# A 16 KB store of zeros to the output ahead of all loads, in a group normalisation kernel bound by DMA

## The chip, the cores and the metric

The kernel runs on 1 core of one Trainium2 chip. The metric is device time in microseconds (us). In the first measurement the kernel before took 635.31 us (median of 3 runs, 635.22 to 635.34).

## The reference, cut to what matters

```python
# x: (128, 1024, 32, 16) bf16;  g, b: (1024,) bf16;  32 groups of 32 channels
xr  = x.reshape(B, 32, 32, H, W)
mu  = xr.mean(axis=(2, 3, 4), keepdims=True)
var = ((xr - mu) ** 2).mean(axis=(2, 3, 4), keepdims=True)
xn  = ((xr - mu) / jnp.sqrt(var + 1e-5)).reshape(B, C, H, W)
return xn * g[None, :, None, None] + b[None, :, None, None]
```

The input has 134.2 MB, and so has the output. Each byte is read once and written once.

## The kernel before

The kernel works on 32 tiles of 4 MB. A tile is 128 rows of 16,384 bf16 elements (32 KB a row): four samples times 32 groups, one group of one sample in each row. A tile is loaded into one of six buffers, its sums are taken on TensorE, its squares on ScalarE (ACT), it is scaled in place on VectorE (DVE), GpSimd (POOL) and ACT, and it is stored from the same buffer. All large loads and stores are issued from SyncE (SP) and go through one queue, q1. Six tiles are loaded ahead; the stores of tiles 0 and 1 come behind those six loads. From there on loads and stores alternate.

```python
XBUFS = 6
UPFRONT = 6
AHEAD = 5
...
    def L(i):                                  # load of tile i
        xt = xpool.tile([P, F], BF16, name="xt")
        parts = NQ if i == 0 or i >= NT - 1 else 1
        w = F // parts
        for c in range(parts):
            chain("sp", nc.sync.dma_start(
                out=xt[:, c * w : (c + 1) * w], in_=x_v[i][:, c * w : (c + 1) * w]))
        state[i] = {"xt": xt}

    for i in range(min(UPFRONT, NT)):
        L(i)

    gb_b = consts.tile([G, 2, KC], BF16)
    chain("act", nc.scalar.dma_start(out=gb_b[:, 0, :], in_=g_v))
    chain("act", nc.scalar.dma_start(out=gb_b[:, 1, :], in_=b_v))
...
    def S(i, lo, hi):                          # store of tile i
        chain("sp", nc.sync.dma_start(
            out=o_v[i][:, lo * QF : hi * QF], in_=state[i]["xt"][:, lo * QF : hi * QF]))
...
    def finish(i):                             # cut: the last two tiles go in parts
        for k in range(KC - LAST_SHARE, KC):
            scale_on("act", i, k)
        S(i, 0, NQ)
        state.pop(i)
        j = i + AHEAD
        if UPFRONT <= j < NT:
            L(j)
```

The `chain` helper only fixes the order on one engine. Line breaks are changed here and the rest is cut.

Of the kernel before, what the change touches and what calls it, by code (L numbers as in the profile page):

```python
# [11 lines left out]
BF16 = mybir.dt.bfloat16  # L12
# [17 lines left out]
def kernel(  # L30
# [13 lines left out]
    nc = tc.nc  # L44
# [11 lines left out]
    MMN = MM_FREE  # L56
# [8 lines left out]
    o_v = out.rearrange("(t n) (g k) h w -> t (n g) (k h w)", n=NS, g=G)  # L65
# [3 lines left out]
    consts = ctx.enter_context(tc.tile_pool(name="consts", bufs=1))  # L69
# [15 lines left out]
    def chain(key, inst):  # L85
        prev = last.get(key)
        if prev is not None:
            tc.add_manual_dep(inst.ins, prev.ins.name, nosync, reason="pipeline order")
        last[key] = inst
        return inst  # L90
# [3 lines left out]
    def L(i):  # L94
# [4 lines that stand above are left out]
            chain(  # L99
                "sp",  # L100
                nc.sync.dma_start(  # L101
                    out=xt[:, c * w : (c + 1) * w], in_=x_v[i][:, c * w : (c + 1) * w]
                ),
            )
        state[i] = {"xt": xt}

    for i in range(min(UPFRONT, NT)):
        L(i)
# [13 lines left out]
        out=eye[:],  # L122
        in_=ones_b[:],
# [8 lines left out]
        out=rep[:].rearrange("q (n a) -> q n a", n=NS),  # L132
        in_=ones_b[0:G, :].rearrange("q (n a) -> q n a", n=NS),
# [274 lines left out]
    def finish(i):  # L408
        if i < 0 or in_parts(i):
            return  # L410
# [7 lines that stand above are left out]
# [42 lines left out]
```

## Time and profile before

| what | before |
|---|---|
| device time, median of all 6 runs | 635.26 us |
| span of the profiled run | 633.4 us |
| busiest compute engine, ACT | 82% |
| bytes moved, mean rate over the span | 268.69 MB, 424 GB/s |
| one 32 KB packet on a DMA engine (median) | 1.21 us |

The page of the kernel before: the busy digits and the rate by slices (40 equal slices of the span; 9 is 90% or more), the DMA queues, and the chain of waits that ended last.

```profile
DMA  9999999999999999999999999999999999999995
GB/s 367 433 431 419 430 431 430 430 433 430 430 434 433 435 431 429 431 430 428 431 435 426 433 439 439 431 426 433 430 435 430 430 435 430 433 423 439 431 418 228
...
q1 hardware_dynamic: 10944, 268.44, 98.8%
q8 instruction: 8, 0.13, 0.1%
q14 instruction: 14, 0.11, 0.0%
q10 hardware_dynamic: 96, 0.00, 0.0%
...
DMA 71%; ACT 10%; PE 9%; DVE 3%; issue 3%; POOL 1%; SPq 0%; DVEq 0%; ACTq 0%; POOLq 0%
```

The DMA engines are full from the second slice to the last but one. So a faster compute engine should not help here; fewer microseconds of DMA time should. The queue lines give packets, MB and share. q10 is ACT's queue and carries only g and b here.

The sum behind this uses the packet records of the trace. 7,680 packets of 32 KB at 1.213 us and 2,048 of 8 KB at 0.309 us, over 16 engines, make 621.8 us of data per engine, starting at 1.8 us.

Two further readings of the trace carry the argument. First, the windows view shows a dip where the six loads ahead end. Its columns are the window, its length, the busy time (and count) of PE, PEld, DVE, ACT and POOL, the TensorE clock, the DMA share, and GB/s. Packets are counted where they start, so short windows swing by some per cent.

```profile
17.00:23.00 6.00, 0.10 (x1) 0.09 (x1) 0.00 (x0) 5.94 (x5) 0.00 (x0) 0.68 1.01 437
58.00:62.00 4.00, 2.21 (x11) 0.78 (x8) 3.56 (x12) 4.00 (x1) 0.00 (x0) 1.00 1.07 377
62.00:68.00 6.00, 3.51 (x9) 1.31 (x10) 1.97 (x4) 5.91 (x4) 2.70 (x6) 0.63 1.01 437
```

The engines are no less busy at 58 to 62 us than before or after, but they move 377 GB/s instead of 437. The packets there take longer: 24 packets that start between 57 and 62.5 us take 1.3 to 3.0 us instead of 1.21, in sum 12.8 us of excess, or 0.8 us per engine. I call these packets the cluster.

Second, the kernel ends with one DMA engine. The sixteen landings of one transfer (each engine's increment of the semaphore) are spread over 0.6 us, from the first to the last, in the pure-load phase and over 8.65 us for the last store. The windows view of the last 20 us shows the engines falling idle one after the other:

```profile
616.00:620.00 4.00, 0.00 (x0) 0.00 (x0) 0.00 (x0) 0.00 (x0) 0.00 (x0) 0.50 1.01 426
620.00:624.00 4.00, 0.00 (x0) 0.00 (x0) 0.00 (x0) 0.00 (x0) 0.00 (x0) 0.50 0.98 416
624.00:628.00 4.00, 0.00 (x0) 0.00 (x0) 0.00 (x0) 0.00 (x0) 0.00 (x0) 0.50 0.44 186
628.00:632.00 4.00, 0.00 (x0) 0.00 (x0) 0.00 (x0) 0.00 (x0) 0.00 (x0) 0.50 0.09 39
```

### The profile page before, as it was taken

To read this page: it belongs to the slowest core of one execution; us is meant where nothing else is said; L and a number is where in the kernel's file an instruction comes from. 1 tells how busy PE (TensorE), PEld (TensorE's weight loads), DVE (VectorE), ACT (ScalarE), POOL (GpSimd) and SP (SyncE) were. 2 spreads that over 40 slices of the span, in tenths; PEclk is the share of its full clock that TensorE was granted. 3 is DMA by queue.
4 is the path that set the end of the run, shared out by engine and by line. 5 is a ranking of instruction groups with operands and counts; after the bars stand their busy time and mean duration, and the time that the engine had idled before them with its cause. 6 is when DMAs were issued, how large, how long until landed. Compare 5 with 4: busy or idle time off the path is not lost.

```text
span 633.4 us, 3906 instructions
## 1 busy us (share of the span) xinstructions
PE 289.4 (46%) x1025; PEld 113.3 (18%) x1025; DVE 368.9 (58%) x825; ACT 518.1 (82%) x238; POOL 228.4 (36%) x373
## 2 busy tenths in 40 slices
PE   5577604663345633456423655235553355547000
PEld 2223201221112211122101222012221122212000
DVE  0077777767744577545675455754557645567760
ACT  4599999999977798777987788977879778797960
POOL 0044444444442244422444333443324433244100
PEclk9789758766787667876668776687866678668655
DMA  9999999999999999999999999999999999999995
GB/s 367 433 431 419 430 431 430 430 433 430 430 434 433 435 431 429 431 430 428 431 435 426 433 439 439 431 426 433 430 435 430 430 435 430 433 423 439 431 418 228
DMA packets 11062, 268.69 MB, mean 424 GB/s; under 512 B 1312, under 2 KB 1312, under 8 KB 1312
## 3 DMA queue, kind: packets, MB, share of 16 engines
q1 hardware_dynamic: 10944, 268.44, 98.8%
q8 instruction: 8, 0.13, 0.1%
q14 instruction: 14, 0.11, 0.0%
q10 hardware_dynamic: 96, 0.00, 0.0%
HBM read 134.22 MB, written 134.22 MB: 424 GB/s over the span
## 4 chain that ended last, share of the span: by engine, by line
DMA 71%; ACT 10%; PE 9%; DVE 3%; issue 3%; POOL 1%; SPq 0%; DVEq 0%; ACTq 0%; POOLq 0%
DMA out_dram<-xt 41%; DMA xt<-in_x_dram 30%; PE pa L166 9%; ACT ja L244 9%; DVE xt L368 3%; ACT xt L363 1%; SPq L101 0%; POOL scl L337 0%; PE pb L166 0%; POOL shift L343 0%; ACT rstd L308 0%; DVE jd L189 0%; DVE rstd L312 0%; POOL bia L353 0%; DVE jv L292 0%
## 5 line engine op out<-in xcount | busy, mean ns | idle before, releaser
L244 ACT ACTIVATE ja<-xt,negmean 128x8192 fp8e5<-128x8192 bf16 x60 | 426.7, 7112 | 74.7 <-DVE jd L189 74.7
L166 PE MATMUL pa<-xt,eye 128*128 128x512 bf16 x976 | 278.6, 456 | 294.6 <-DMA xt<-in_x_dram 294.6
L368 DVE TENSOR_SCALAR xt<-xt,scl,bia 128x512 bf16<-128x512 bf16 x716 | 341.3, 552 | 39.8 <-POOL bia L353 39.8
L166 PEld LDWEIGHTS <-eye 128*128 128x128 bf16 x1024 | 113.2, 113 | 470.8 <-DMA xt<-in_x_dram 295.9
L368 POOL TENSOR_SCALAR xt<-xt,scl,bia 128x512 bf16<-128x512 bf16 x240 | 190.5, 805 | 3.3
L337 POOL TENSOR_SCALAR scl<-gb,rstd 128x32 f32<-128x32 f32 x31 | 11.1, 358 | 337.0 <-DVE rstd L312 337.0
L189 DVE TENSOR_SCALAR_CACHE_REDUCE jd<-pa 128x512 bf16<-128x512 f32 x32 | 22.0, 688 | 172.3 <-PE pa L166 172.3
L363 ACT ACTIVATE xt<-xt,bia,scl 128x512 bf16<-128x512 bf16 x68 | 50.8, 798 | 0.8 <-DVE bia L324 0.8
L244 ACT ACTIVATE ja<-xt,q 128x4096 fp8e5<-128x4096 bf16 x8 | 29.7, 3708 | 7.0 <-DVE jd L189 6.8
L312 DVE RECIPROCAL rstd<-rstd 128x1 f32<-128x1 f32 x32 | 5.1, 160 | 24.6 <-ACT rstd L308 24.6
L343 POOL TENSOR_SCALAR shift<-scl,negmean 128x32 f32<-128x32 f32 x31 | 11.1, 358 | 3.1
L166 PE MATMUL pb<-xt,eye 128*128 128x512 bf16 x48 | 11.0, 379 | 1.0 <-DMA xt<-in_x_dram 1.0
L244 ACT ACTIVATION_READ_ACCUMULATOR ja<-xt,negmean 128x1 f32 x60 | 11.2, 186 | 0.0
L308 ACT ACTIVATE rstd<-s,v 128x1 f32<-128x1 f32 x30 | 8.8, 295 | 2.8
L353 POOL TENSOR_TENSOR bia<-shift,gb 128x32 f32<-128x32 f32 x31 | 7.8, 251 | 2.6
L216 POOL TENSOR_SCALAR off<-negmean,q 128x1 f32<-128x1 f32 x2 | 0.9, 430 | 20.6 <-DVE jd L189 20.6
L308 ACT ACTIVATE rstd<-var,eps_t 128x1 f32<-128x1 f32 x2 | 0.6, 294 | 7.5 <-DVE jv L292 7.5
L273 POOL TENSOR_SCALAR v<-s 128x1 f32<-128x1 f32 x30 | 5.7, 191 | 2.5
L156 DVE COPY gb<-gb_p 128x64 f32<-128x64 f32 x1 | 0.2, 225 | 5.3 <-PE gb_p L148 5.3
L116 ACT ACT_TABLE_LOAD x1 | 1.3, 1283 | 1.7 <-PEq L444 1.7
L189 DVE DVE_READ_ACCUMULATOR jd<-pa 128x1 f32 x32 | 2.6, 81 | 0.0
L292 DVE TENSOR_SCALAR_CACHE_REDUCE jv<-sq,seed 128x4 f32<-128x4 f32 x2 | 0.4, 216 | 2.9 <-ACT ja L244 2.9
(18 smaller groups left out, 6.1 us busy)
## 6 DMA issues: line engine op xcount, KB each, us to landing
xt<-in_x_dram SPq DMA_DIRECT2D x30, 4096.0 KB, 29.2
out_dram<-xt SPq DMA_DIRECT2D x30, 4096.0 KB, 38.3
xt<-in_x_dram SPq DMA_DIRECT2D x8, 1024.0 KB, 16.4
out_dram<-xt SPq DMA_DIRECT2D x8, 1024.0 KB, 18.8
gb_b<-in_g_dram ACTq DMA_DIRECT2D x1, 2.0 KB, 3.4
gb_b<-in_b_dram ACTq DMA_DIRECT2D x1, 2.0 KB, 5.4
```

Of the source, the lines that this page charges most:

```text
L116: chain("act", nc.scalar.activation(out=warm[:], in_=eps_t[:], func=ACT.Sqrt))
L166: nc.tensor.matmul(out=ps[:], lhsT=eye[:], rhs=st["xt"][:, k * MMN : (k + 1) * MMN], start=(k == lo), stop=(k == hi - 1),),
L189: nc.vector.tensor_scalar(out=jd[:], in0=ps[:], scalar1=-inv_n, scalar2=seed, op0=ALU.mult, op1=ALU.add, accum_out=total[:],),
L244: nc.scalar.activation(out=ja[:, 0:w], in_=st["xt"][:, k * w : (k + 1) * w], func=ACT.Square, bias=bias, scale=scale, accum_out=sq, satura ...
L273: nc.gpsimd.tensor_scalar(out=v0[:], in0=s0[:], scalar1=inv_n, scalar2=EPS, op0=ALU.mult, op1=ALU.add,),
L308: nc.scalar.activation(out=rstd[:], in_=last_sum[:], func=ACT.Sqrt, bias=bias[:], scale=scale),
L312: chain("dve", nc.vector.reciprocal(out=rstd[:], in_=rstd[:]))
L337: nc.gpsimd.tensor_scalar(out=scl[:], in0=gam, scalar1=rstd[:], scalar2=None, op0=ALU.mult),
L343: nc.gpsimd.tensor_scalar(out=shift[:], in0=scl[:], scalar1=st["negmean"][:], scalar2=None, op0=ALU.mult,),
L353: nc.gpsimd.tensor_tensor(out=bia[:], in0=shift[:], in1=bet, op=ALU.add),
L363: inst = nc.scalar.activation(out=span, in_=span, func=ACT.Identity, bias=bia, scale=scl)
L368: inst = eng.tensor_scalar(out=span, in0=span, scalar1=scl, scalar2=bia, op0=ALU.mult, op1=ALU.add,)
```

## The change

The intent, as read from the diff: if the first write to the output costs something once, pay it with a tiny store before the loads start, where it might be hidden. The zeros are overwritten by the result of tile 0.

```diff
         state[i] = {"xt": xt}
+
+    zero = consts.tile([16, MMN], BF16)
+    nc.vector.memset(zero[:], 0.0)
+    chain("act", nc.scalar.dma_start(out=o_v[0][0:16, 0:MMN], in_=zero[:]))
 
     for i in range(min(UPFRONT, NT)):
         L(i)
```

## The prediction

> **What bounds the kernel now.** The page gives a DMA busy share of nine tenths or more in every slice but the last, and only 82% for the busiest compute engine (ACT). The chain that ended last is 71% DMA. The DMA packet records of the trace say it more exactly. A packet of 32 KB takes 1.21 us (median) and one of 8 KB 0.31 us; 7,680 and 2,048 of them over 16 DMA engines are (7680 x 1.21 + 2048 x 0.31)/16 = about 621 us per engine. The first data packet starts at 1.8 us. The 16 landings (semaphore increments) of each transfer are 0.6 us apart in the pure-load phase, but 8.7 us apart for the last store: one engine is a straggler and ends the kernel. It gains about 1 us of lag at each of the eight instruction-fetch packets of 16 KB (0.95 to 1.07 us each); its other lag dates from 54 to 61 us. In the windows view the rate falls away from 623 us.
>
> **What the change can touch.** The loads run at a constant 9.71 us per 4 MB on each engine until the first store. The first store's turn comes at about 58 to 60 us: 24 packets there take 1.3 to 3.0 us instead of 1.21. Its landing step is 10.2 us on the fast engines (+0.5), 10.4 in the mean (+0.7) and about 11.4 to 11.8 on the two slowest (+1.7 to +2.0, of which an instruction fetch is about 1 on one). No later store shows such a step on all engines at once. So a first write to the output costs each engine a one-time 0.5 to 1 us, on the critical path because the DMA engines never idle.
>
> **What it adds.** One DVE memset (estimate 0.1 us; the 128x128 one took 0.17), one ACT issue of about 0.42 us, and 16 packets of 1 KB, one per engine (0.04 us each, scaled from 0.31 per 8 KB). It delays g and b by about 0.6 us; they landed by 6.6 us at the latest and GB's matmul runs at 15.0, so this is slack. The first store gains a wait on a DMA done long before; the ACT table load has slack to 10 us. The Trainium skill, "DMA: Bandwidth & Descriptors", section "Issuing engines are not separate DMA queues", says that queues share the same 16 engines and interleave; in this trace q1 and q10 do at 2 to 6 us. So a stall of the small store can hold loads up too: the cost is partly moved, not removed. The first loads already stall there (8 KB packets of 0.4 to 1.06 us at 1.8 to 2.5 us), so part should overlap.
>
> **Sum.** Removed: about 0.7 us at 58 us (up to 1 on the straggler). Added at the start: 0.1 to 0.7 us. Net estimate: 0.4 us faster, 634.9 us.
>
> **What would show it.** Right: no cluster of packets over 1.3 us at the first store, its landing step near 9.7 us, the first 1 MB load landing no more than 0.3 us later, the straggler's end about 0.4 us earlier with the other engines alike. Wrong, case a: the cluster stays, so it is load-to-store turnaround or many addresses, and the time is unchanged or 0.1 us longer. Case b: the cluster goes but the early loads land 0.5 to 0.7 us later, and the time is unchanged.
>
> **What would make it wrong.** A changed placement of instruction fetches among engines, or a different skew in the steady state, could move the end by 1 us either way.

## The result and the profile after

After: 635.13 us, median of 6 runs (634.84 to 635.67). Before, in the same rounds and the first measurement: 635.26 us. The ratio is 0.9999, with a 95% interval of 0.9987 to 1.0012. Ratios here are not quite the ratios of the medians quoted.

The matching lines of the page after:

```profile
DMA  9999999999999999999999999999999999999995
GB/s 365 430 437 418 430 431 430 432 431 436 430 435 432 422 433 431 429 430 430 433 432 438 430 432 434 429 430 432 432 436 432 432 434 430 434 421 440 431 415 216
...
q1 hardware_dynamic: 10944, 268.44, 98.7%
...
q10 hardware_dynamic: 128, 0.02, 0.0%
...
DMA 73%; PE 9%; ACT 8%; DVE 3%; issue 3%; SPq 0%; POOL 0%; DVEq 0%; ACTq 0%; POOLq 0%
```

q10 has 32 packets more: 16 of data and 16 semaphore writes. The Trainium skill, "DMA: Bandwidth & Descriptors", section "Why a DMA increments its semaphore by 16 and not by 1", says that the size of the slowest dimension sets how many engines a DMA uses; 16 rows give 16 engines. This trace agrees.

What was added is visible in the timeline of the first microseconds after (start, duration, engine, line, operation):

```profile
0.79 2.54 SPq L101 DMA_DIRECT2D xt<-in_x_dram  x5
0.90 0.27 DVE L108 MEMSET zero<- 16x256 uint32 x1 [0.90 <-PEq L448]
1.21 0.39 ACTq L109 DMA_DIRECT2D out_dram<-zero  x1
...
2.70 1.28 ACT L120 ACT_TABLE_LOAD   x1 [2.70 <-issue]
```

The loads start first, at 0.79 us as before, since the store waits for its memset. ACT's table load comes 1.0 us later than before (2.70 against 1.70 us), in slack. The store's data packets ran from 4.8 to 5.2 us, among those of the loads: "ahead of all loads" is true of the program's text, not of the queue. Each took 0.046 us, so none of them met a stall.

The same windows of the kernel after:

```profile
17.00:23.00 6.00, 0.18 (x1) 0.10 (x1) 0.00 (x0) 5.93 (x5) 0.27 (x1) 0.59 1.01 437
58.00:62.00 4.00, 2.49 (x12) 0.94 (x10) 4.00 (x13) 4.00 (x2) 0.04 (x1) 1.00 1.07 385
62.00:68.00 6.00, 3.52 (x17) 1.64 (x18) 1.56 (x6) 5.91 (x4) 1.58 (x4) 1.00 1.01 437
...
624.00:628.00 4.00, 0.00 (x0) 0.00 (x0) 0.00 (x0) 0.00 (x0) 0.00 (x0) 0.50 0.44 184
628.00:632.00 4.00, 0.00 (x0) 0.00 (x0) 0.00 (x0) 0.00 (x0) 0.00 (x0) 0.50 0.11 47
```

The dip is still there, 385 GB/s, with 25 packets over 1.3 us. The end looks the same too: the last store's landings have a mean of 626.53 us after and 626.49 us before.

**A correction that the landings force.** The prediction says that the slow packets come with the first store. They do not belong to it. In the trace of before, the load of tile 5 lands between 61.6 and 64.5 us, and the first store between 71.5 and 74.2 us. The cluster lies at 58 to 62 us. On most engines it is the last one or two of the eight packets of the last load ahead of the store. The store's own packets, from about 61.3 us on, take 1.21 us from the first one. (Following one engine's packets is a reconstruction: a packet is put behind the one that ends where it starts.) Whether the store behind causes the stall had to be tested.

### The profile page after: what moved, and what is told of

Same layout as the page of the kernel before. It is cut to its first block, busy times and chain, and to the rows that moved or that the text cites. A ratio compares the mean times of both kernels' runs of the same rounds, so it can differ in the third digit from the quotient of the medians. Undisturbed runs are those within 1.5% of the kernel's fastest.

```text
span 633.8 us, 3908 instructions
## 1 busy us (share of the span) xinstructions
PE 290.6 (46%) x1025; PEld 113.5 (18%) x1025; DVE 369.8 (58%) x826; ACT 518.0 (82%) x238; POOL 229.4 (36%) x373
## 4 chain that ended last, share of the span: by engine, by line
DMA 73%; PE 9%; ACT 8%; DVE 3%; issue 3%; SPq 0%; POOL 0%; DVEq 0%; ACTq 0%; POOLq 0%
DMA out_dram<-xt 47%; DMA xt<-in_x_dram 26%; PE pa L170 9%; ACT ja L248 7%; DVE xt L372 3%; ACT xt L367 1%; SPq L101 0%; DVE jd L193 0%; POOL scl L341 0%; ACT rstd L312 0%; DVE rstd L316 0%; DVE jv L296 0%; POOL shift L347 0%; DVEq L459 0%; POOL bia L357 0%
```

## The experiments

The measures, all from the traces' packet records and landings:

- "cluster": packets of 32 KB that take over 1.3 us, and the sum of their time over 1.213 us, in the window named;
- "step": mean landing of a transfer over its 16 engines, minus that of the transfer before it. A 4 MB transfer alone has 9.71 us, and about 9.8 when an instruction packet falls on one of its engines.

| run | what was added or moved | cluster at 57 to 62.5 us | step of the last load ahead of the first result store | median us (before, same chip) | ratio, 95% interval |
|---|---|---|---|---|---|
| before | – | 24 packets, 12.8 us | 10.42 | 635.26 | |
| c0_before | nothing (control) | 20, 12.7 us | 10.42 | 635.36 (one run) | |
| after | 16 KB ahead, ACT queue | 25, 10.9 us | 10.35 | 635.13 | 0.9999, 0.9987–1.0012 |
| e1_wide | 128 KB ahead, ACT queue | 16, 6.9 us | 10.09 | 635.64 (635.16) | 1.0009, 0.9992–1.0025 |
| e2_sp | 16 KB ahead, SP queue | 27, 13.3 us | 10.49 | 636.53 (635.16) | 1.0019, 1.0004–1.0034 |
| e3_mid | 128 KB behind the second load, issued early | 22, 10.8 us | 10.34 | 635.83 (635.16) | 1.0009, 0.9994–1.0024 |
| e4_up5 | five loads ahead, not six | 0; 27, 15.8 us at 48 to 52 us | 10.57 | 636.01 (635.16) | 1.0014, 0.9997–1.0030 |
| e5_junk4m | 4 MB behind the second load | 1; 32, 22.8 us at 18 to 23 us | 9.71 | 645.70 (635.50) | 1.0158, 1.0143–1.0173 |
| e6_junk1m | 1 MB behind the second load | 0; 32, 24.8 us at 18 to 23 us | 9.77 | 638.43 (635.50) | 1.0044, 1.0029–1.0059 |
| e9_late128k | 128 KB behind the second load, issued later | 25, 12.6 us | 10.48 | 635.75 (635.54) | 1.0005, 0.9990–1.0020 |
| e11_lateload | a load issued late, no store added | 24, 14.2 us | 10.43 | 635.61 (635.54) | 1.0002, 0.9985–1.0018 |
| e13_start1m | 1 MB ahead, ACT queue | 1 | 9.78 | 638.22 (635.31) | 1.0045, 1.0032–1.0059 |

The 0.7 us at stake is below what the times resolve (about 1 us between runs), so the traces decide the mechanism. Each kernel was profiled once; only the kernel before was profiled twice. All results were correct.

The theories: A, a first write costs once per stretch of the output; C, it costs once per queue; D, it is a fixed time or the compute; B, E and F, it is the turn from loads to stores, any such turn or only the first; P, the first DMA that is issued late.

**c0_before: how far does the cluster vary?** No edit.

> The kernel before, unchanged, profiled once more: how far does the cluster vary from profile to profile? Expected: 20 to 30 packets over 1.3 us at 58 to 61.5 us and a landing step of the last load ahead of the first store of 10.3 to 10.5 us; the 16-row store's 10.35 us against 10.42 is then no difference.

Measured: 20 packets and again 10.42 us. The 10.35 us of the change is a difference of 0.07 us. Runs whose edit is not thought to matter (e2, e9, e11) span 10.43 to 10.49, so 0.07 us is of the size of the scatter and I read nothing into it.

**e1_wide: touch all 128 rows of the first tile.**

```diff
+    zero = consts.tile([P, MMN], BF16)
+    nc.vector.memset(zero[:], 0.0)
+    chain("act", nc.scalar.dma_start(out=o_v[0][:, 0:MMN], in_=zero[:]))
```

> The zero store is widened from 16 rows (1 KB each) to all 128 rows of the first result tile, still on the ScalarE queue, before the loads. Theory A (one-time first write, paid per engine and per stretch of the output): the 16-row store left most of the stretches untouched, so now the cluster of some 25 packets over 1.3 us at 58 to 61.5 us should be gone (under 5 left) and the step of the landings there falls from 10.4 to about 9.75 us. Theory B (it is the turn from pure loads to stores, or something else at that time, and no early small write matters): the cluster stays with 20 to 30 packets and 9 to 13 us of excess. Time: within 0.5 us of before under both; early loads 0.2 to 0.4 us later.

Measured: the cluster did not go, but it was the smallest of all the kernels that kept it: 16 packets, and a step of 10.09 us. Neither theory's numbers were met. The load of tile 1 landed 0.48 us later (mean 23.05 against 22.57 us), of which about 0.31 us is the bytes (2.48 us for 1 MB, divided by 8). So perhaps 0.3 us was prepaid and 0.2 us of it paid at the start; this is one profile, and no gain is left.

**e2_sp: the same 16 KB on the SP queue.**

```diff
+    zero = consts.tile([16, MMN], BF16)
+    nc.vector.memset(zero[:], 0.0)
+    chain("sp", nc.sync.dma_start(out=o_v[0][0:16, 0:MMN], in_=zero[:]))
```

> The 16 KB store moves to the SyncE queue, ahead of the loads there. Theory C (the first store costs once per queue, and ScalarE's queue was the wrong one): cluster at 58 to 61.5 us gone. Theories A and B: it stays with 20 to 30 packets. The loads are issued after a wait for the memset and one more issue, so everything is 0.4 to 0.9 us later and the time about 0.5 us longer (635.8).

Measured: cluster unchanged, so theory C falls, for a store of this size (e13_start1m below settles it for a large one). The loads now wait for the memset: their landings come 0.83 us later all along (23.40 against 22.57 us), and the median is 1.4 us longer than that of before.

**e3_mid: a small store in the middle of the loads.**

```diff
     for i in range(min(UPFRONT, NT)):
         L(i)
+        if i == 1:
+            chain("sp", nc.sync.dma_start(out=o_v[0][:, 0:MMN], in_=zero[:]))
```

(The tile of zeros is made as in e1_wide.)

> A 128-row store of zeros (128 KB) goes on the SyncE queue between the second and third tile's loads, so that its turn comes in the middle of the pure-load phase at about 22 us. Theory A (first write): a cluster of slow packets (over 1.3 us) at about 20 to 23 us, and none at 58 to 61.5 us. Theory B1 (any turn from load to store): a cluster at 20 to 23 us and another at 58 to 61.5 us. Theory B2 (only a full-rate stretch of stores does it, or a fixed point in time): nothing at 22 us, cluster stays at 58 to 61.5 us. Time within 0.6 us of before.

Measured: at 22 us nothing happens. The first write of the whole execution, on all 16 engines and into all 128 rows of the first tile, takes 0.05 us a packet; its step is 0.35 us and the next load's 9.68 us, so the engines lost nothing but the bytes. The cluster stays at 58 us. This ends theory A: a first write, as such, costs nothing here, and having touched the rows does not help. It also ends B1, that any turn to a store, however small, does it. The windows of this run, to be set beside those of before (437 and 377 GB/s):

```profile
17.00:23.00 6.00, 0.10 (x1) 0.10 (x1) 0.00 (x0) 5.94 (x5) 0.00 (x0) 0.71 1.08 459
58.00:62.00 4.00, 2.73 (x13) 1.06 (x11) 3.71 (x12) 4.00 (x1) 0.00 (x0) 1.00 0.99 352
```

**e4_up5: one load fewer ahead of the first store.**

```diff
-UPFRONT = 6
+UPFRONT = 5
```

> No zero store; one load fewer goes ahead of the first result store, so that store follows 20 MB of loads instead of 24 MB in the queue and has its turn about 9.7 us earlier, at 51 to 53 us. Theories A, B1 and B2a (the stall belongs to the first result store or the turn to stores): the cluster moves to 48.5 to 52 us. Theory D (a fixed time after the start, or something that compute does at 58 to 60 us): the cluster stays at 58 to 61.5 us. The time is within 2 us of before.

Measured: the cluster moved with the store, to 48 to 52 us. Theory D falls. The windows view of this run:

```profile
48.00:52.00 4.00, 4.00 (x20) 1.67 (x18) 1.53 (x4) 3.91 (x4) 2.27 (x5) 1.00 0.91 287
58.00:62.00 4.00, 4.00 (x20) 1.77 (x19) 4.00 (x13) 4.00 (x1) 0.00 (x0) 1.00 1.05 451
```

The same two windows have 393 and 377 GB/s before; the first of them there (the second is shown above) is

```profile
48.00:52.00 4.00, 4.00 (x19) 1.61 (x17) 1.98 (x4) 3.91 (x4) 2.71 (x6) 1.00 0.91 393
```

The stall goes where the six (now five) loads end and the first store begins, although the store itself is issued at about the same time.

**e5_junk4m and e6_junk1m: a real stretch of stores in the middle of the loads.** The raw input tile 0 is stored and later overwritten.

```diff
     for i in range(min(UPFRONT, NT)):
         L(i)
+        if i == 1:
+            chain("sp", nc.sync.dma_start(
+                out=o_v[0][:, 0:w], in_=state[0]["xt"][:, 0:w]))   # w = F, or QF
```

> A full 4 MB store (the raw first tile, overwritten later by the result) goes between the second and third tile's loads on the SyncE queue, with packets of 32 KB as the results have. Theory E (the stall of about 0.7 us per engine belongs to a turn from a pure stretch of loads to a full stretch of stores, every time): a cluster of 15 to 30 slow packets at 19 to 22 us, and a second one at the first result store, now at about 68 to 71 us. Theory F (it is a one-time cost of the first full-size store): a cluster at 19 to 22 us only, and under 6 slow packets at 68 to 71 us. Time: 9.7 us of added packets, so about 645 us.

> The same with 1 MB (8 KB packets), between the second and third loads. The cost of its packets is 2.5 us of the queue, so about 637.7 us. Under theory E a stall of 0.4 to 0.8 us in the landing step at 22 us, and the cluster at the first result store (now 61 to 64 us) stays. Under theory F the cluster there shrinks to under 6 packets if 1 MB is enough to pay the one-time cost. If neither place changes against the 128 KB store (no stall at 22 us, cluster stays), the size of the packets or of the stretch decides.

Measured: in both, the stall comes at the junk store (32 packets at 18 to 23 us, a step of 11.0 and 11.1 us for the load ahead of it), and the first result store, some 40 to 50 us later, has none (steps of 9.71 and 9.77 us, and no slow packet at 66 to 74 us in e5 or at 60 to 66 us in e6). So theory F holds for these runs and E, a stall at every turn, falls: it is paid at the first turn to a large store and not again. In before, the store of tile 1 goes to addresses that nothing in the execution wrote earlier, and the turn back to loads follows it at about 81 us; yet from 62.5 to 86 us not one packet is slow. So it is not a cost of fresh addresses either. The windows of the 4 MB run, then of the 1 MB run:

```profile
17.00:23.00 6.00, 0.00 (x0) 0.00 (x0) 0.00 (x0) 5.94 (x5) 0.00 (x0) 0.52 1.03 344
68.00:74.00 6.00, 5.13 (x22) 2.11 (x21) 2.95 (x6) 5.91 (x4) 3.68 (x7) 0.96 1.00 431
...
17.00:23.00 6.00, 0.00 (x0) 0.00 (x0) 0.00 (x0) 5.93 (x5) 0.00 (x0) 0.54 1.04 339
58.00:62.00 4.00, 3.95 (x20) 1.81 (x19) 4.00 (x13) 4.00 (x3) 0.35 (x2) 1.00 0.95 410
62.00:68.00 6.00, 3.41 (x17) 1.39 (x16) 1.55 (x6) 5.91 (x4) 1.18 (x4) 1.00 0.99 426
```

They have 344 and 339 GB/s at 17 to 23 us, where before has 437. But nothing was saved: the stall costs 1.3 to 1.4 us per engine at 22 us and 0.7 us at 60 us. The 1 MB run's load of tile 5 lands 3.04 us later than before, for 2.48 us of bytes.

**e7_up4: let the queue run empty ahead of the first store.**

```diff
-UPFRONT = 6
+UPFRONT = 4
...
-        j = i + AHEAD
-        if UPFRONT <= j < NT:
-            L(j)
+        for j in range(UPFRONT, AHEAD + 1) if i == 0 else (i + AHEAD,):
+            if UPFRONT <= j < NT:
+                L(j)
```

> Only four tiles are loaded ahead of the first result store; the queue runs empty at about 42 us and the store is issued at 45 us. If the stall belongs to stores (theories E, F), the last load packets at 39 to 43 us run at 1.21 us and the store's own first packets at 46 to 49 us are slow. If it belongs to the end of a stretch of loads (theory G), packets at 39 to 42 us are slow with no store behind them. The queue's gap of about 3 us should make the time about 638 us.

Measured: neither place. The last packets of the loads (39 to 42 us) run at 1.22 us, which ends theory G. The store's own first packets, from 47.3 us, run at 1.21 to 1.27 us. The slow packets are the store's eighth, at 55.8 us, and the first ones of the load right behind it, at 57.5 us (29 in all), and then 21 more at 74 to 78 us, ahead of the second store:

```profile
48.00:54.00 6.00, 5.30 (x22) 2.11 (x20) 2.74 (x5) 5.91 (x4) 3.47 (x7) 0.90 1.02 437
54.00:59.00 5.00, 0.00 (x0) 0.00 (x0) 5.00 (x10) 5.00 (x5) 4.06 (x6) 0.70 0.93 316
59.00:63.00 4.00, 0.00 (x0) 0.00 (x0) 3.81 (x12) 4.00 (x1) 0.00 (x0) 0.50 1.16 500
63.00:74.00 11.00, 5.56 (x16) 2.07 (x17) 6.74 (x11) 10.91 (x7) 7.38 (x12) 0.54 1.01 435
74.00:78.00 4.00, 3.74 (x17) 1.53 (x16) 4.00 (x14) 4.00 (x2) 0.15 (x1) 1.00 0.88 311
```

So the first seven packets an engine gets of a full 4 MB store, with no load beside them, pay nothing. The slow packets stand where loads and stores are adjacent in a running queue: here first from store to load, then from load to store. Taken with the other runs, I read the stall as one of an early turn between large loads and large stores, after which turns are free. That it came twice here fits no theory that I had. The median was 640.95 us (ratio 1.0081, interval 1.0064 to 1.0098), mostly for the empty queue, which moved no data from about 41.7 us (42.9 us on one engine) to 47.3 us.

**e9_late128k and e11_lateload: is it the first DMA that is issued late?** In e5 and e6 the store waited for data and so was issued late; in e3 it was not.

```diff
+        if i == 1:        # e9_late128k, in the loop of loads
+            chain("sp", nc.sync.dma_start(
+                out=o_v[0][:, 0:MMN], in_=state[0]["xt"][:, 0:MMN]))
```

```diff
-    for i in range(min(UPFRONT, NT)):          # e11_lateload
+    for i in range(min(UPFRONT - 1, NT)):
         L(i)
...
         chain("dve", nc.vector.reciprocal(out=rstd[:], in_=rstd[:]))
+        if i == 0:
+            chain("dve", nc.vector.tensor_copy(out=scr2[:], in_=scr[:]))
+            chain("sp", nc.sync.dma_start(out=scr[:], in_=x_v[0][:, 0:16]))
+            L(UPFRONT - 1)
```

> A 128 KB store (128 rows of 1 KB) between the second and third loads as in the earlier mid-queue run, but of raw input, so that it is issued only after the first tile has landed (13 us) instead of at 3 us. Theory P (the stall comes with the first DMA that is issued late, while the queue is already running, whatever its size): a stall in the landing steps at 22 us (1 to 1.5 us over the 9.71 plus 0.3 us of its bytes) and no cluster at the first result store. Theory S (it takes a store of at least about 1 MB, or packets above 1 KB): as in the earlier run, nothing at 22 us and the cluster at 58 to 61.5 us.

> No extra store. The sixth tile's load is issued late, at about 33 us, after a small load (4 KB) that waits for VectorE's work on the first tile; until then five loads are queued, to 52 us. Theory P (first late issue, load or store): slow packets at 48 to 52 us, ahead of the late load, and none at 58 to 62 us ahead of the first result store. Theory S (turn to stores): no slow packets at 48 to 52 us, cluster at 58 to 62 us as in before. Time within 0.6 us of before.

Measured: theory P falls. The late load (issued at 34.0 us, its turn from about 51.6 us) has no slow packet ahead of it, and the cluster stays at the store. The 128 KB store was issued at 5.7 us, not 13 as expected, since it needs only the first quarter of the tile; it waited for data all the same, its step was 0.34 us, two packets at 1.3 us stood ahead of it, and the cluster at 58 us stayed. In the same place 1 MB brings the stall and takes it away from the later place; 128 KB does neither.

**e10_early1m: 1 MB of zeros, issued early.** This one did not build; the tile of zeros did not fit beside the six buffers.

> 1 MB of zeros (two stores of 128 rows of 4 KB) in the same place, issued early, with the first loads, with nothing to wait for. Theory P: no stall at 19 to 24 us, cluster at the first result store (61 to 64 us) as in before. Theory S: cluster or stall of about 1.3 us at 19 to 24 us and none at the first result store. Time: 2.5 us of bytes, so about 638 us either way.

**e13_start1m: the change, scaled up until it works.** The zeros lie in an input buffer, so that they fit.

```diff
+    zero = xpool.tile([P, F], BF16, name="xt")
+    nc.vector.memset(zero[:, 0:QF], 0.0)
+    chain("act", nc.scalar.dma_start(out=o_v[0][:, 0:QF], in_=zero[:, 0:QF]))
+
     for i in range(min(UPFRONT, NT)):
         L(i)
```

> The change scaled up: 1 MB of zeros (8 KB packets, the size that worked in the middle of the queue) on the ScalarE queue ahead of the loads, from the first input buffer, which the sixth load reuses. If an early store of enough bytes prepays the stall: under 6 slow packets at 60 to 65 us and a step near 9.75 us there. Its bytes cost 2.5 us. If the stall is hidden behind the start of the loads, the end comes 1.8 us later than before (637.2 us); if it is only moved, 2.5 to 3.2 us later (637.9 to 638.6 us). If the cluster stays, the stall is not to be prepaid before the loads at all.

Measured: it does prepay. One slow packet is left at 57 to 62.5 us, and it is beside an instruction fetch; the step of the last load is 9.78 us.

```profile
58.00:62.00 4.00, 3.95 (x19) 1.84 (x19) 4.00 (x10) 4.00 (x5) 2.08 (x4) 1.00 1.12 483
```

But the price is paid at the start. The load of tile 1 lands 3.36 us later than before (25.93 against 22.57 us); 2.48 us of that is the bytes, so 0.9 us more was lost there, which I take for the stall, against 0.7 us saved at 60 us. The load of tile 5 lands 2.70 us later, and the median is 2.9 us longer than that of before. The windows view shows the price at the start, in before and then in this run:

```profile
2.00:14.00 12.00, 7.71 (x28) 3.12 (x28) 0.70 (x2) 5.17 (x5) 0.00 (x0) 1.00 1.04 430
2.00:14.00 12.00, 5.33 (x16) 2.05 (x17) 1.90 (x5) 5.64 (x5) 0.56 (x2) 1.00 0.98 370
```

The 1 MB went through ACT's queue and freed the stores of SP's queue from the stall, so what is paid once is not kept per queue (theory C for a large store). The delay of the loads agrees with the Trainium skill, "DMA: Bandwidth & Descriptors", section "Issuing engines are not separate DMA queues", by which DMAs run on the same 16 engines and interleave, whichever engine issued them: the store was issued by ACT and the loads by SP, and still the loads gave way by all of its bytes and 0.9 us more.

**e8_split: a try at the straggler.** One late store was cut so that the engines get unequal shares.

```diff
+SKEWED = (24,)
...
+        for p0, p1 in ((0, 120), (120, P)) if i in SKEWED else ((0, P),):
+            chain("sp", nc.sync.dma_start(
+                out=o_v[i][p0:p1, lo * QF : hi * QF],
+                in_=state[i]["xt"][p0:p1, lo * QF : hi * QF]))
```

> One late result store (tile 24) is split into rows 0 to 119 and 120 to 127. By the Trainium skill's page on DMA, section on how many engines a DMA uses, the first part should use 15 engines and the second 8, so the sixteenth engine gets no packet of this tile (9.7 us less), eight engines get one packet more (1.2 us). Theory H (the kernel's end is one straggling engine, and it is the sixteenth): the spread of the last landings falls from 8.7 us to about 7 us and the time falls by 1 to 1.5 us. If the straggler is one of the lowest eight: its end is 1.2 us later, time about 636.5 us. If it is engine 8 to 14: no change of the end.

Measured: 639.96 us against 635.50 (ratio 1.0062, interval 1.0047 to 1.0077), 4.5 us longer, and a spread of the last landings of 11.5 us. No listed outcome fits. The trace shows the split as expected, with 15 landings of the first part and 8 of the second. One engine lands the next load at 527.5 us, 10.6 us ahead of the second; this must be the one without a share. One tile time (9.7 us) earlier, at 517.8 us, lies among the first landings of the load before (517.0 to 524.7 us), so this engine was not the straggler. What made the run longer is the split store itself: 107 packets of 32 KB that start at 517 to 546 us take 1.3 to 3.0 us (none does in before), 5.1 us of excess per engine. In two slices of the page the rate fell to 401 and 333 GB/s. Why these packets are slow was not followed up.

No run beat both kernels.

## Why the prediction was right, and where it was not

- **The total.** Predicted 634.9 us, with up to 1 us either way left open. Measured 635.13 us. This agreement is luck as far as the mechanism goes: a forecast of 0.4 us lies within the scatter of the times (about 1 us), so the total would have been met whether the stall went or stayed. The forecast gain of 0.4 us is not confirmed: the ratio is 0.9999, and the mean landing of the last store, which does not depend on one straggler, is 626.53 us after and 626.49 before. The right reading is no gain.
- **What bounds the kernel.** Right: DMA time from start to end, then one straggling engine. In all, 621.8 us of packets per engine from 1.8 us on stand against an end at 632.4 us (before, last landing).
- **"A first write to the output costs each engine a one-time 0.5 to 1 us."** This is the step that failed. The size (0.7 us in the mean) held, and so did "one-time", but for e7_up4; "a first write" did not. e3_mid's first write was free and prepaid nothing. The stall is at the first turn between large loads and large stores in the running queue. The slow packets are mostly the last packets of the load ahead; I had counted one transfer too few in the order of landings and so gave them to the store.
- **"Removed: about 0.7 us at 58 us."** Mis-sized by all of it: 25 packets against 24, 10.35 us against 10.42, within the scatter. This is the prediction's own "case a": the cluster stays.
- **"Added at the start: 0.1 to 0.7 us."** The measured cost lies below its lower end: the 16 packets took 0.046 us each, and the load of tile 1 lands at 22.60 us in the mean against 22.57. (The memset took 0.27 us, not the estimated 0.1, without effect.)
- **"A stall of the small store can hold loads up too: the cost is partly moved, not removed."** It did not arise with 16 KB, as there was no stall. With 1 MB it did: 0.9 us at the start against 0.7 us saved (e13_start1m).
- **What was only argued.** Which part of the hardware stalls, why the stall is paid once (twice in e7_up4), and where between 128 KB and 1 MB the threshold lies, or whether it is the size of the packet (1 KB against 8 KB and more) that counts, are open. The size of the store and that of its packets were changed together. e1_wide suggests a gradual effect for a store ahead of the loads.

The straggler is a matter apart from the change, but it is the larger reserve: its last landing is 5.9 us behind the mean of the sixteen (632.4 against 626.5 us). The prediction says that it gains about 1 us at each of the eight packets of q8 (16 KB, 0.95 to 1.07 us each). The landings do not bear this out. The last landing of a transfer does move away from the first at the packet of 37.7 us (from 0.59 to 1.66 us), but the distance stays at 5.1 us across the packet of 256.7 us, at 5.9 across 334.9, at 6.9 across 414.0 and at 7.9 across 568.8. From 200 us on it grows by 0.7 to 1.0 us at a time, in the transfers into which 8 KB packets of q14 fall, at 225, 313, 402, 499 and 593 to 595 us; each takes 0.31 us, and a 32 KB packet that starts as it ends takes 1.4 to 1.9 us. The traces of c0_before and after show the same. So late in the kernel the lag goes with packets of q14, which the page calls "instruction" too, and not with those of q8. Whose they are the trace does not tell.

As for q8, the Trainium skill, "Runtime: NRT & Kernel Launch", section "Instruction fetch mechanics", says that a sequencer fetches its instructions in blocks of 16 KiB, 256 instructions, through its own DMA queue. TensorE has 2,050 matmuls and weight loads, which make eight such blocks (2050/256 = 8.0), and the packets of q8 from the second on come 77 to 79 us apart, the time of four tiles with 64 of them each. So these fetches are probably TensorE's; no run here changed their number.

## What to carry to other kernels

A one-time cost seen at the first store need not be a cost of the first write: look at whose packets are slow, by the order of landings, before building a remedy on it. A queue that is full gave nothing away here (e5, e6, e13): the stall could be moved, but the DMA engines were busy at both places, so moving it saved nothing, and every byte of the trick cost its time. When the effect at stake is smaller than the scatter of the times, let the trace decide, and profile the unchanged kernel twice to know what the trace can tell apart.

## What the Trainium skill lacked or had wrong

- "DMA: Bandwidth & Descriptors" has no word of a one-time stall where a running queue first turns between large loads and large stores: 0.7 us per engine at 60 us (step of 10.42 instead of 9.71 us), 1.3 to 1.4 us at 22 us, none at the later turns except in e7_up4, where it came twice. A store of 128 KB in mid-queue does not cause it; one of 1 MB does.
- "Runtime: NRT & Kernel Launch", section "Instruction fetch mechanics", calls the cost of crossing a block "mostly hidden" and does not speak of the DMA engine that carries the fetch. In this kernel, bound by DMA, that engine loses the time: a 16 KB packet took 0.95 to 1.07 us, and at the first one the last landing of a transfer moved from 0.59 to 1.66 us behind the first. Whether TensorE waited for a fetch no run here shows.
- "DMA: Bandwidth & Descriptors", section "Rules for kernel authors", asks for 128 partitions but does not say what a split into 120 and 8 rows costs: one such 4 MB store made the kernel 4.5 us longer, with 107 packets of 1.3 to 3.0 us instead of 1.21.
